# Fused attention and feed-forward block on Trainium2: three edits to which engine prepares the weights, the first softmax tiles and the first scale

## The chip, the cores and the metric

The kernel runs on one core of a Trainium2 chip. The core has a matrix engine (TensorE, PE in the profile, with its weight loads shown apart as PEld), three elementwise engines (VectorE or DVE, ScalarE or ACT, GpSimd or POOL) and a queue from which the DMAs are issued (SyncE or SP). Each engine runs its own instructions in the order in which they stand in its queue. The metric is the device time of one launch in microseconds; lower is better.

## What is computed

The reference, cut to what matters:

```python
scores = (1 / sqrt(64)) * q @ k.T            # q, k, v: 8 batches, 8 heads, 576 rows, 64 columns
thresh = max(scores, axis=-1) - tau
attn = exp(where(scores >= thresh, scores, -1e9) - max)
attn = attn / (sum(attn) + 1e-9)
x = (attn @ v), heads side by side           # 4608 rows of 512
h = x @ w_in                                 # 512 x 2048
out = (h * sigmoid(h)) @ w_out               # 2048 x 512
```

Everything is float32. The kernel gets the accuracy out of 16-bit products by carrying a number as a first part and a second part (the first rounded to float16, the second what the rounding left), and multiplying first by first, first by second and second by first. For that, weights, v and softmax weights are scaled by powers of two ahead of the split.

## The kernel before, in words

**Tiles.** The softmax works on tiles of 128 query rows by 576 keys. The program writes one loop over tile numbers t. In each step it writes the maximum of tile t (`soft1`, line 434, VectorE), the scores of tile t+1 (TensorE, line 412 or 424), the normalisation of tile t-1 (`soft2b`, line 466, ScalarE), the exponential of tile t (`soft1b`, line 444, ScalarE), what is done with the normalised tile t-1 (`soft3`), the tasks planned for step t, units of the feed-forward products, and the threshold, sum and reciprocal of tile t (`soft2`, lines 453, 457, 461, VectorE).

**Batch 0 in two halves.** Batch 0 is computed for the query rows 0 to 255 of each head first. These are 16 tiles, called direct tiles here (they are the visits of kind "low"): their scores, transposes (line 369) and products with v (`av_direct`, line 389) are done in float32 on TensorE. Then come twelve empty steps (`GAP`), then the other 20 tiles of batch 0 (kind "high"), then batches 1 to 7. All tiles but the direct ones are split into float16 parts: the first part by ScalarE up to step 36 (line 475) and by GpSimd after that (line 477), the second part by GpSimd (lines 480 and 483). A DMA then transposes both parts (line 493), and TensorE multiplies them with the split v (line 508).

**Weights.** There are 16 pieces of w_in and 16 of w_out, 128 rows by 512 columns each. They come as 64-bit words, are loaded into two staging buffers (w_in partly into eight other ones), and are decoded by ScalarE (line 191) and VectorE (lines 194 and 197). TensorE multiplies each decoded piece with itself (line 209); the largest entry of the sums bounds the square of the largest weight, and VectorE reads it (line 214). When all 16 pieces of a matrix have gone through this, `pow2_scales` turns the bound into a power of two (lines 111 to 149), and `split_weights` scales each piece (line 220, GpSimd), writes its first part (line 223, ScalarE) and its second (line 224, GpSimd). The parts of piece i lie where the raw piece i-2 lay, so that the split of piece i waits until that of piece i-2 is done.

**v.** v of a batch is loaded in four pieces (line 245). VectorE takes the largest absolute value of each (`vmax`, line 251), `pow2_scales` makes the scale (its square-root branch, lines 123 to 136, is for the weights alone), and `split_v` splits each piece (ScalarE line 288, VectorE line 289). From the scale of batch 0 also comes `xscale` (line 263), by which the direct products are scaled when they leave PSUM (lines 526 and 527).

**Feed-forward.** x is split and multiplied with w_in (`h_unit`, line 551); tanh, gate and split of the result run on ScalarE and VectorE (lines 559, 560, 566, 567); the product with w_out is `o_unit` (line 582), and the result leaves through ScalarE (line 592).

**What sets the order.** `at(step, task)` plans a task for a step. `W_PLAN` plans the weights: w_in is loaded and decoded in steps 0 to 10 and split in steps 10 to 12; w_out is decoded in steps 9 to 22 and split in steps 22 to 25, with a priority that puts its instructions ahead of 150 of the preceding ones. The framework then orders the instructions of each engine by priority and by the times of its own model of the chip; the order on the chip is fixed by that. So the position of an instruction in its engine's queue in the trace need not be that of its step. PSUM holds two score tiles, three banks for other products (two in rotation, one of which the weights' products and some scales use under the number 2), and one for the products with v.

Of the kernel before, what the change touches and what calls it, by code (L numbers as in the profile page):

```python
# [10 lines left out]
BF16 = mybir.dt.bfloat16  # L11
F32 = mybir.dt.float32
F32R = mybir.dt.float32r
I32 = mybir.dt.int32
AF = mybir.ActivationFunctionType
ALU = mybir.AluOpType
AX = mybir.AxisListType
PSUM = bass.MemoryType.PSUM

P = 128  # L20
# [3 lines left out]
NK = DM // P  # L24
# [28 lines left out]
def attention_moe(  # L53
# [10 lines left out]
    nc = tc.nc  # L64
    const = ctx.enter_context(tc.tile_pool(name="const", bufs=1))
# [12 lines left out]
    def bank(shape, name, own=None):  # L78
        if own is None:
            own = turn[0] = (turn[0] + 1) % turn[1]  # L80
        return ps_m.tile(shape, F32, tag=f"m{own}", name=name)
# [7 lines left out]
        out=gate, in0=tau_sb, scalar1=0.0, scalar2=0.125, op0=ALU.is_ge, op1=ALU.mult  # L89
# [3 lines left out]
        out=ntau, in0=tau_sb, scalar1=0.0, scalar2=-1.0, op0=ALU.max, op1=ALU.mult  # L93
# [6 lines left out]
    for i in range(2):  # L100
        t = const.tile([P, S + 64], F32R, name=f"qstack{i}")
# [4 lines left out]
    def pow2_scales(mx, name, own=None, squared=False):  # L106


        k = name[0]
        one = const.tile([P, 1], F32, name=f"{name}_one", tag=f"{k}_one")  # L110
        nc.vector.tensor_reduce(out=one, in_=mx, op=ALU.max, axis=AX.X)
        diag = const.tile([P, P], BF16, name=f"{name}_diag", tag="diag")
        nc.scalar.activation(diag, ident, AF.Copy, scale=one)
        allp = bank([P, P], f"{name}_ps", own)
        nc.tensor.matmul(allp, ones, diag, start=True, stop=True)
        one = const.tile([P, 1], F32, name=f"{name}_all", tag=f"{k}_all")
        nc.vector.tensor_reduce(out=one, in_=allp, op=ALU.max, axis=AX.X)
        cl = const.tile([P, 1], F32, name=f"{name}_cl", tag=f"{k}_cl")
        low, high = (2.0**-40, 2.0**94) if squared else (2.0**-20, 2.0**47)
        nc.vector.tensor_scalar(  # L120
            out=cl, in0=one, scalar1=low, scalar2=high, op0=ALU.max, op1=ALU.min
        )
        if squared:
            twice = const.tile([P, 1], F32, name=f"{name}_twice", tag=f"{k}_twice")
            nc.vector.tensor_scalar(
                out=twice, in0=cl, scalar1=2.0, scalar2=None, op0=ALU.mult
            )
            half = const.tile([P, 1], I32, name=f"{name}_half", tag=f"{k}_half")
            nc.vector.tensor_scalar(
                out=half, in0=twice.bitcast(I32), scalar1=1, scalar2=EXPMASK,  # L130
                op0=ALU.logical_shift_right, op1=ALU.bitwise_and,
            )
            cl = const.tile([P, 1], F32, name=f"{name}_root", tag=f"{k}_root")
            nc.vector.tensor_scalar(
                out=cl, in0=half.bitcast(F32), scalar1=2.0**64, scalar2=None, op0=ALU.mult
            )
        e2 = const.tile([P, 2], I32, name=f"{name}_e2", tag=f"{k}_e2")
        nc.vector.tensor_scalar(
            out=e2[:, 0:1], in0=cl.bitcast(I32), scalar1=EXPMASK, scalar2=None, op0=ALU.bitwise_and
        )  # L140
        nc.vector.tensor_scalar(
            out=e2[:, 1:2], in0=cl.bitcast(I32), scalar1=EXPMASK, scalar2=EXPMASK,
            op0=ALU.bitwise_and, op1=ALU.bitwise_xor,
        )
        sc = const.tile([P, 2], F32, name=f"{name}_sc", tag=f"{k}_sc", bufs=3)
        nc.vector.tensor_scalar(
            out=sc[:, 0:1], in0=e2[:, 1:2].bitcast(F32), scalar1=2.0**12, scalar2=None, op0=ALU.mult
        )
        nc.vector.tensor_scalar(
            out=sc[:, 1:2], in0=e2[:, 0:1].bitcast(F32), scalar1=2.0**-13, scalar2=None, op0=ALU.mult  # L150
        )
        return sc
# [4 lines left out]
    w16 = wst.bitcast(F16)  # L157
# [58 lines left out]
    def split_weights(i):  # L216
        w = wst[:, i + WSPARE, :]
        hi = w16[:, i, 0:512]
        sc = wsc["in" if i < 4 * NK else "out"][:, 0:1]
        nc.gpsimd.tensor_scalar(  # L220
            out=w, in0=w, scalar1=sc, scalar2=1.0, op0=ALU.mult, op1=ALU.mult
        )
        nc.scalar.activation(hi, w, AF.Copy)
        nc.gpsimd.tensor_tensor(
            out=w16[:, i, 512:1024], in0=w, in1=hi, op=ALU.subtract
        )
# [11 lines left out]
    vmx = {}  # L238
    vsc = {}
    v16 = {}  # L240
    vraw = {}

    def load_v(b, p):
        t = sb.tile([P, 2, 5, D], F32, tag="vraw", name=f"vraw_{b}_{p}", bufs=5)
        nc.sync.dma_start(out=t, in_=vL[b, :, 2 * p : 2 * p + 2])
        vraw[b, p] = t

    def vmax(b, p):
        if p == 0:
            vmx[b] = const.tile([P, NPAIR], F32, name=f"vmx_{b}", tag="vmx")  # L250
        nc.vector.tensor_reduce(
            out=vmx[b][:, p : p + 1], in_=vraw[b, p], op=ALU.max, axis=AX.XYZ,
            apply_absolute_value=True,
        )
# [3 lines left out]
    xscale = const.tile([P, 1], F32, name="xscale")  # L258

    def vscale(b):  # L260
        vsc[b] = pow2_scales(vmx[b], f"v{b}", (None, 2)[b] if b < 2 else 0)
        if b == 0:
            nc.vector.tensor_scalar(
                out=xscale, in0=vsc[0][:, 0:1], scalar1=2.0**-12, scalar2=None, op0=ALU.mult
            )
# [76 lines left out]
    direct = {}  # L342
    qzero = []
    for i in range(2):
        t = gbuf.bitcast(F32)[:, 4096 + 512 * i : 4608 + 512 * i]
# [55 lines left out]
    tiles = []  # L401
# [61 lines left out]
    def soft2b(t):  # L463
        w = wtile[t]
        r = small.pop(t)[:, 4:5]
        nc.scalar.activation(w, w, AF.Copy, scale=r)  # L466

    def soft3(t):
        if tiles[t][0] in direct:
# [162 lines left out]
    start = {}  # L632
# [38 lines left out]
    for b in range(B):  # L671
        u = start[b, 0]
        for p in range(NPAIR):
            if b == 0:
                at(-4, lambda p=p: load_v(0, p))
                at(0, lambda p=p: vmax(0, p))
                at(V_SLOT + p, lambda p=p: split_v(0, p))
            else:
                at(u + 9 * p - 40, lambda b=b, p=p: load_v(b, p))
                at(u + 9 * p - 34, lambda b=b, p=p: vmax(b, p))  # L680
                at(u + 9 * p + 4, lambda b=b, p=p: split_v(b, p))
        at(u - 2 if b else 1, lambda b=b: vscale(b))
# [16 lines left out]
    for first, t0, t1, t2, hp in W_PLAN:  # L699
        for i in range(16):  # L700
            ti = t0 + i * (t1 - t0) / 16
            at(math.floor(ti - 2), pri(hp, lambda i=i + first: load_weights(i)))
            at(math.floor(ti), pri(hp, lambda i=i + first: decode_weights(i)))
        at(t1, pri(hp, scale_out if first else scale_in))
        for i in range(16):
            at(t1 + i * (t2 - t1) // 16, pri(hp, lambda i=i + first: split_weights(i)))
# [26 lines left out]
    t = 0  # L733
    while t < NT + 8 or units or ready or held:
        while ready and ready[0][0] <= t:
            _, b, c0, n = ready.pop(0)
# [14 lines left out]
        if live(t - 1):  # L751
            soft2b(t - 1)
# [14 lines left out]
        for v, p, c0, n in avs.pop(t, []):  # L767
            b = visits[v][0]
# [5 lines left out]
            scale = xscale if v in direct else 2.0**-12  # L774
# [52 lines left out]
```

## Time and profile before

| | us |
|---|---|
| median of three runs | 1242.41 |
| lowest and highest | 1241.87, 1245.1 |
| the profiled execution, its own time | 1240.96 |
| span of the profile of that execution | 1238.8 |

The profile shows one execution. Its span runs from the first to the last instruction; 2.2 us of the execution's time lie outside. Engines are shown by their busy time; an instruction that waits for an input shows as idle time of its engine, and the trace names what released it. "x" is a count. PEclk is the granted clock of TensorE as a share of full speed. In a group of one source line, three numbers with slashes are the shortest, median and longest duration in ns.

The later stages look alike: from 250 us on TensorE is busy for more than 94% of each stretch, with softmax tiles of the batches 1 to 7 and feed-forward units side by side. The first 250 us hold everything that the change touches.

### The profile page before, as it was taken

The numbers are of one execution on the slowest core, as the hardware profiler recorded it, in microseconds if no ns is written. First come the engines' busy times: TensorE is split into PE (matmuls) and PEld (weight loads), VectorE is DVE, ScalarE is ACT, GpSimd is POOL, SyncE is SP. The second block draws the span as 40 slices with busy tenths as digits, with TensorE's granted clock in tenths as the row PEclk, the third lists the DMA queues.
The fourth block names the chain that finished last, engine by engine and source line by source line (L and its number), as shares of the span: only waits on it lengthen the run. The fifth ranks groups of instructions, "written<-read, shape, count | busy, mean of one in ns | idle before, by whom it ended". The sixth has DMA issues, their size and how long they took to land.

```text
span 1238.8 us, 26929 instructions
## 1 busy us (share of the span) xinstructions
PE 1142.8 (92%) x9402; PEld 896.8 (72%) x9402; DVE 931.1 (75%) x2603; ACT 814.8 (66%) x1507; POOL 748.6 (60%) x952
## 2 busy tenths in 40 slices
PE   5776766999899999999999999999999999999998
PEld 3544545777678778777777877787777877777777
DVE  7898866797989998989888859887689848333230
ACT  6888656687677867776777747776677847433331
POOL 1088999788678867886788618783688537200000
PEclk9997887999999999999999999999999999999999
DMA  9669556877878877788787648773688446200000
GB/s 303 183 208 207 129 98 131 158 135 151 163 129 151 160 150 146 154 144 162 141 153 148 123 99 146 157 148 88 118 162 154 83 79 112 52 15 15 14 12 24
DMA packets 363479, 158.15 MB, mean 128 GB/s; under 512 B 329552, under 2 KB 338256, under 8 KB 363344
## 3 DMA queue, kind: packets, MB, share of 16 engines
q1 hardware_dynamic: 363344, 156.43, 62.3%
q8 instruction: 74, 1.21, 0.4%
q14 instruction: 61, 0.50, 0.1%
HBM read 66.72 MB, written 9.44 MB: 61 GB/s over the span
## 4 chain that ended last, share of the span: by engine, by line
PE 64%; DVE 13%; DMA 8%; POOL 5%; ACT 5%; issue 3%; SPq 1%; POOLq 0%; ACTq 0%; DVEq 0%
PE h L551 23%; PE o L582 23%; PE s L424 10%; PE a L508 8%; DMA wT<-hl 3%; DVE w L453 3%; DVE sm L434 3%; DMA vraw<-in_vL 2%; DVE qstack L328 2%; POOL hl L480 2%; ACT w L444 2%; DVE v L289 1%; DMA wraw<-in_w_out 1%; POOL hl L477 1%; ACT w L466 1%
## 5 line engine op out<-in xcount | busy, mean ns | idle before, releaser
L551 PE MATMUL h<-x,wst 128*128 128x288 f16 (+2 forms) x3072 | 430.9, 289 | 14.0 <-DVE gbuf L567 12.0
L582 PE MATMUL o<-gbuf,wst 128*128 128x288 f16 (+2 forms) x3072 | 426.2, 288 | 4.9 <-ACT wst L592 2.5
L551 PEld LDWEIGHTS <-wst 128*128 128x128 f16 x3072 | 292.6, 99 | 102.8 <-issue 22.1
L582 PEld LDWEIGHTS <-wst 128*128 128x128 f16 x3072 | 294.5, 99 | 89.5 <-issue 9.1
L480 POOL TENSOR_TENSOR hl<-w,hl 128x512 f16<-128x512 f32 x272 | 325.3, 1196 | 15.7 <-DMA kraw<-in_kT 3.5
L477 POOL TENSOR_SCALAR hl<-w 128x576 f16<-128x576 f32 x264 | 178.8, 680 | 198.4 <-ACT w L466 128.3
L444 ACT ACTIVATE w<-s,sm 128x576 f32<-128x576 f32 x288 | 210.1, 737 | 81.4 <-DVE sm L434 33.8
L453 DVE SCALAR_TENSOR_TENSOR w<-s,sm,w 128x576 f32<-128x576 f32 x288 | 232.5, 812 | 41.4 <-ACT w L444 39.4
L466 ACT ACTIVATE w<-w,sm 128x576 f32<-128x576 f32 x288 | 218.4, 771 | 58.4 <-DVE sm L461 56.5
L434 DVE TENSOR_REDUCE sm<-s 128x1 f32<-128x576 f32 x288 | 215.0, 750 | 42.8 <-PE s L424 41.0
L560 DVE SCALAR_TENSOR_TENSOR h<-th,h 128x288 f32<-128x288 f32 (+2 forms) x256 | 116.5, 456 | 114.5 <-ACT th L559 112.0
L559 ACT ACTIVATE th<-h,msc 128x288 f32<-128x288 f32 (+2 forms) x256 | 126.9, 497 | 105.4 <-PE h L551 103.0
L424 PE MATMUL s<-khi,qstack 128*128 128x288 f32 x608 | 160.6, 346 | 31.3 <-DVE w L453 27.2
L566 ACT ACTIVATE gbuf<-h 128x288 f16<-128x288 f32 (+2 forms) x256 | 103.7, 407 | 81.6 <-DVE h L560 80.5
L567 DVE SCALAR_TENSOR_TENSOR gbuf<-h,gbuf 128x288 f16<-128x288 f32 (+2 forms) x256 | 114.9, 451 | 40.8 <-ACT gbuf L566 39.8
L508 PE MATMUL a<-wT,v 128*64 128x288 f16 (+1 forms) x1680 | 128.7, 295 | 10.2 <-DMA wT<-hl 10.2
L424 PEld LDWEIGHTS s<-khi,qstack 128*128 128x128 f32 x608 | 98.6, 197 | 53.8 <-issue 42.1
L338 POOL TENSOR_TENSOR klo<-kraw,khi 128x576 fp32r<-128x576 f32 x64 | 92.5, 1446 | 71.3 <-ACT khi L336 71.3
L424 PE MATMUL s<-klo,qstack 128*128 128x288 f32 x608 | 133.7, 302 | 0.0
L508 PEld LDWEIGHTS <-v 128*64 128x64 f16 x1680 | 91.3, 111 | 37.0 <-issue 25.0
L424 PEld LDWEIGHTS s<-klo,qstack 128*128 128x128 f32 x608 | 101.5, 196 | 0.5 <-issue 0.2
L483 POOL TENSOR_TENSOR hl<-w,hl 128x64 f16<-128x64 f32 x272 | 101.7, 374 | 0.0
(93 smaller groups left out, 830.6 us busy)
## 6 DMA issues: line engine op xcount, KB each, us to landing
qraw<-in_qT SPq DMA_DIRECT2D x128, 144.0 KB, 3.0
kraw<-in_kT SPq DMA_DIRECT2D x128, 144.0 KB, 3.1
vraw<-in_vL SPq DMA_DIRECT2D x32, 320.0 KB, 3.4
wraw<-in_w_out SPq DMA_DIRECT2D x16, 512.0 KB, 4.4
out_t<-wst SPq DMA_DIRECT2D x56, 144.0 KB, 2.2
wT<-hl SPq DMA_TRANSPOSE x304, 3.4
gbuf<-in_w_in SPq DMA_DIRECT2D x8, 512.0 KB, 7.5
wraw<-in_w_in SPq DMA_DIRECT2D x8, 512.0 KB, 6.0
```

The source lines that it names most:

```text
L424: nc.tensor.matmul(s_ps[:, j, :HALF], lhs, kk[:, j * HALF : (j + 1) * HALF], start=(n == 0), stop=(n == len(seq) - 1),)
L434: nc.vector.tensor_reduce(out=negm, in_=s_ps[:, :, :HALF], op=ALU.max, axis=AX.XY, negate=True)
L444: nc.scalar.activation(wtile[t].rearrange("p (j c) -> p j c", j=2), sps[t][:, :, :HALF], AF.Exp, bias=small[t][:, 0:1],)
L453: nc.vector.scalar_tensor_tensor(out=w3, in0=s_ps[:, :, :HALF], scalar=sm[:, 1:2], in1=w3, op0=ALU.is_ge, op1=ALU.mult, accum_out=sm[:, 2:3],)
L466: nc.scalar.activation(w, w, AF.Copy, scale=r)
L477: nc.gpsimd.tensor_scalar(out=fl[:, 0:S], in0=w, scalar1=1.0, scalar2=1.0, op0=ALU.mult, op1=ALU.mult)
L480: nc.gpsimd.tensor_tensor(out=fl[:, 640:1152], in0=w[:, 0:512], in1=fl[:, 0:512], op=ALU.subtract)
L508: nc.tensor.matmul(a_ps[odd * D : (odd + 1) * D, :n], vt[:, lo_v, odd, kv, :], wT[v, b * H + 2 * p + odd][:, kw, c0 - base : c0 - base + n ...
L551: nc.tensor.matmul(ph[:, :n], wi(c, f, lo_w), x16[b, lo_x][:, c, c0 : c0 + n], start=(k == 0), stop=(k == 11),)
L559: nc.scalar.activation(th[:, :n], ph[:, :n], AF.Tanh, scale=moe_sc[b][:, 0:1])
L560: nc.vector.scalar_tensor_tensor(out=ph[:, :n], in0=th[:, :n], scalar=1.0, in1=ph[:, :n], op0=ALU.add, op1=ALU.mult,)
L582: nc.tensor.matmul(ps[:, :n], wo(f, d, lo_w), g[:, lo_g, :n], start=(f == 0 and k == 0), stop=(f == NF - 1 and k == 2),)
```

## The change

It has three edits.

1. In `split_weights`, the pieces of w_out are no longer scaled by GpSimd. ScalarE writes the first part with the scale applied on the way, and VectorE writes the second part from the raw piece, the scale and the first part. The pieces of w_in keep the old three instructions.
2. In `soft2b`, the direct tiles (16 of batch 0) are normalised by GpSimd, in place, instead of ScalarE. All others stay.
3. In `vmax`, for batch 0, TensorE multiplies the upper halves of the words of v with themselves (20 products, into a PSUM bank under the number 2), and VectorE reduces the sum once; the four reductions over the pieces are gone. `vscale` for batch 0 takes the square-root branch of `pow2_scales`, three more small instructions. Batches 1 to 7 keep line 251.

No DMA is added, removed or planned for another step.

```diff
@@ split_weights
         sc = wsc["in" if i < 4 * NK else "out"][:, 0:1]
+        if i >= 4 * NK:
+            nc.scalar.activation(hi, w, AF.Copy, scale=sc)
+            nc.vector.scalar_tensor_tensor(
+                out=w16[:, i, 512:1024], in0=w, scalar=sc, in1=hi, op0=ALU.mult, op1=ALU.subtract
+            )
+            return
         nc.gpsimd.tensor_scalar(
             out=w, in0=w, scalar1=sc, scalar2=1.0, op0=ALU.mult, op1=ALU.mult
         )
@@ vmax
+    vps = []
+
     def vmax(b, p):
+        if b == 0:
+            if p == 0:
+                vps.append(bank([P, P], "vps_0", 2))
+            flat = vraw[b, p].rearrange("p o k d -> p (o k d)").bitcast(BF16)
+            upper = flat.rearrange("p (c t) -> p c t", t=2)[:, :, 1]
+            for j in range(5):
+                part = upper[:, j * P : (j + 1) * P]
+                nc.tensor.matmul(
+                    vps[0], part, part, start=(p == 0 and j == 0), stop=(p == 3 and j == 4)
+                )
+            if p == 3:
+                vmx[b] = const.tile([P, 1], F32, name="vmx_0", tag="vmx0")
+                nc.vector.tensor_reduce(out=vmx[b], in_=vps[0], op=ALU.max, axis=AX.X)
+            return
@@ vscale
-        vsc[b] = pow2_scales(vmx[b], f"v{b}", (None, 2)[b] if b < 2 else 0)
+        vsc[b] = pow2_scales(
+            vmx[b], f"v{b}", (None, 2)[b] if b < 2 else 0, squared=(b == 0)
+        )
@@ soft2b
-        nc.scalar.activation(w, w, AF.Copy, scale=r)
+        if tiles[t][0] in direct:
+            nc.gpsimd.tensor_scalar(
+                out=w, in0=w, scalar1=r, scalar2=1.0, op0=ALU.mult, op1=ALU.mult
+            )
+        else:
+            nc.scalar.activation(w, w, AF.Copy, scale=r)
```

## The prediction

> **What bounds the kernel now.** I read the page first, for the engines over the whole span and in 40 slices of 31 us.
>
> ```profile
> span 1238.8 us, 26929 instructions
> PE 1142.8 (92%) x9402; PEld 896.8 (72%) x9402; DVE 931.1 (75%) x2603; ACT 814.8 (66%) x1507; POOL 748.6 (60%) x952
> ...
> PE   5776766999899999999999999999999999999998
> ...
> DVE  7898866797989998989888859887689848333230
> ...
> POOL 1088999788678867886788618783688537200000
> PEclk9997887999999999999999999999999999999999
> ```
>
> TensorE is the bound as a whole, but not at the start: its first seven slices are below 8, its granted clock falls there too, and from the eighth slice on it is nearly full. The work of TensorE is the same before and after but for 20 small products. So what is saved in the first 250 us arrives at the end, because behind them TensorE has hardly a gap to lose it in. The windows of that start come next; the columns are the stretch, then busy time and count of PE, PEld, DVE, ACT and POOL, the clock, the DMA share and GB/s.
>
> ```profile
> 15.00:66.00 51.00, 40.35 (x237) 27.06 (x237) 47.45 (x138) 44.92 (x86) 3.42 (x3) 0.93 0.76 232
> 66.00:100.00 34.00, 22.23 (x141) 14.89 (x137) 30.82 (x77) 28.23 (x54) 32.71 (x35) 0.86 0.71 200
> 100.00:138.00 38.00, 28.96 (x208) 23.27 (x209) 31.37 (x91) 32.48 (x65) 34.39 (x35) 0.76 0.96 192
> 138.00:210.00 72.00, 45.88 (x315) 35.46 (x312) 48.91 (x129) 43.88 (x77) 68.45 (x82) 0.84 0.55 111
> 210.00:250.00 40.00, 34.74 (x290) 26.73 (x289) 31.32 (x87) 25.67 (x45) 31.11 (x42) 0.95 0.77 149
> 300.00:400.00 100.00, 94.26 (x779) 73.21 (x779) 90.10 (x258) 74.61 (x135) 75.86 (x99) 0.97 0.79 150
> ```
>
> There are two different stages. From 15 to 66 us, with the direct tiles, VectorE is busy 47.45 of 51 us (0.930), ScalarE 44.92, GpSimd almost not. From 138 to 210 us GpSimd is busy 68.45 of 72 us, and VectorE only 48.91. The chain of waits says the same of the second stage (start, us, what), with the timeline's row for the long run of GpSimd and the GpSimd time of lines 220 and 224 alone in that window:
>
> ```profile
> 137.13 0.93 POOL hl L480
> ...
> 142.02 7.97 POOL wst L220 x11
> ...
> 166.31 1.06 POOL hl L480
> 167.37 5.09 DMA wT<-hl
> ...
> 178.44 3.58 DVE v L289
> ...
> 217.63 4.98 DMA wT<-hl
> ```
>
> ```profile
> 142.00 11.79 POOL L220 TENSOR_SCALAR wst<-wst,o_w_sc 128x512 f32<-128x512 f32 x15
> ```
>
> ```profile
> 138.00:210.00 72.00, 12.48 (x16) 0.84 0.55 111
> ```
>
> ```profile
> 138.00:210.00 72.00, 18.29 (x16) 0.84 0.55 111
> ```
>
> From 137 to 167 us the chain hardly leaves GpSimd. In its middle stand 15 scalings of w_out in a row. They were released together by w_out's scale and went ahead of the float16 splits of the softmax tiles, for which the DMA transposes and then TensorE wait.
>
> **Edit 1, w_out.** It takes 12.48 + 18.29 = 30.77 us of GpSimd out of this stage, which leaves 68.45 - 30.77 = 37.68. ScalarE keeps its 16 first parts. VectorE gets 16 operations with two operands in SBUF. The trace has this form at line 197, of the same 512 elements, and at line 289 with 640. Line 194 has one operand. Each is shown here for the stretch in which GpSimd idles (0 to 66 us) and for a later one in which GpSimd is busy (66 to 138, for line 289 138 to 230); the three numbers are shortest, median and longest in ns:
>
> ```profile
> L194 DVE TENSOR_SCALAR wst<-wst x19: 405/416/428, 12.3 to 65.0; 128x512 int32<-128x512 int32 x19
> ```
>
> ```profile
> L194 DVE TENSOR_SCALAR wst<-wst x13: 404/753/1369, 68.5 to 125.2; 128x512 int32<-128x512 int32 x13
> ```
>
> ```profile
> L197 DVE SCALAR_TENSOR_TENSOR wst<-wraw,wst x11: 677/681/691, 21.5 to 65.5; 128x512 int32<-128x512 int32 x11
> ```
>
> ```profile
> L197 DVE SCALAR_TENSOR_TENSOR wst<-wraw,wst x14: 682/1089/1642, 65.5 to 125.7; 128x512 int32<-128x512 int32 x14
> ```
>
> ```profile
> L289 DVE SCALAR_TENSOR_TENSOR v<-vraw,v_sc,v x4: 869/870/874, 32.3 to 36.1; 128x640 f16<-128x640 f32 x4
> ```
>
> ```profile
> L289 DVE SCALAR_TENSOR_TENSOR v<-vraw,v_sc,v x4: 868/1272/3568, 143.3 to 199.3; 128x640 f16<-128x640 f32 x4
> ```
>
> So a second part costs VectorE between 0.681 and 1.089 us. GpSimd would be busy about 37.7 of some 65 us, 58%; 0.681 + 0.58 x 0.408 = 0.918, and 16 of them are 14.7 us (ends 10.9 and 17.4). Less GpSimd also gives something back: the four splits of v took 0.868 + 2 x 1.272 + 3.568 = 6.98 us, where undisturbed ones take 4 x 0.870 = 3.48, so 3.5 us go. VectorE then has 48.91 + 14.7 - 3.5 = 60.1 us of work and becomes the bound of the stage. How full can it be? Where it set the pace (15 to 66 us) it was 0.930 full: 60.1 / 0.930 = 64.6 us instead of 72, **7.4 us less**. The ends are 0.826 (31.37 of 38, from 100 to 138 us), which gives 72.8 and no gain, and 1, which gives 60.1 and 11.9 us. I take 0.930, because the stretch at 0.826 also had GpSimd 90% busy.
>
> The edit adds a wait: the ScalarE part of piece i waits for the VectorE part of piece i-2, and the VectorE part for the ScalarE part. Behind them in the two queues stand exponentials and tanh, and the maxima and gates; TensorE waits for these. The plan's priority puts all 16 early, so VectorE may run them as one block of some 15 us, as GpSimd does its 15 scalings now. In the sum that block is VectorE work like other work; its price beyond that is a rival below.
>
> From 210 to 250 us TensorE was 34.74 of 40 us busy, against 94.26 of 100 later. The chain still passes a DMA transpose at 217.63, late because the splits before it were late. At the later pace 34.74 would take 36.9: between 0 and 3.1 us, and I take **2.5 less**, as the cause goes away.
>
> **Edits 2 and 3, the direct tiles.** Their rows: the start of the timeline, and the groups of the operations concerned (busy us, mean ns of one).
>
> ```profile
> 6.22 2.45 DVE L251 TENSOR_REDUCE vmx<-vraw 128x1 f32<-128x640 f32 x3 [3.21 <-DMA vraw<-in_vL]
> ...
> 6.29 4.21 PE L412 MATMUL s<-kd,gbuf 128*128 128x288 f32 x8 [6.29 <-ACT gbuf L361]
> ...
> 10.78 1.41 DVE L434 TENSOR_REDUCE sm<-s 128x1 f32<-128x576 f32 x2
> ...
> 13.49 0.61 PE L209 MATMUL wps<-wst 128*128 128x128 bf16 x4 [2.99 <-DVE wst L197]
> ```
>
> ```profile
> 67.99 11.84 POOL L220 TENSOR_SCALAR wst<-wst,i_w_sc 128x512 f32<-128x512 f32 x15
> ```
>
> ```profile
> 78.39 0.76 ACT L466 ACTIVATE w<-w,sm 128x576 f32<-128x576 f32 x1
> ```
>
> ```profile
> L466 ACT ACTIVATE w<-w,sm 128x576 f32<-128x576 f32 x288 | 218.4, 771 | 58.4 <-DVE sm L461 56.5 <-DVE v_e L138 1.4
> ...
> L477 POOL TENSOR_SCALAR hl<-w 128x576 f16<-128x576 f32 x264 | 178.8, 680 | 198.4 <-ACT w L466 128.3 <-DMA wT<-hl 45.7 <-DVE h L560 17.8
> ...
> L214 DVE TENSOR_REDUCE wmx<-wps 128x1 f32<-128x128 f32 x8 | 2.2, 278 | 0.0
> ...
> L125 DVE TENSOR_SCALAR i_w_twice<-i_w_cl 128x1 f32<-128x1 f32 x1 | 0.1, 145 | 0.0
> ```
>
> *Scale of v.* The four reductions lie at 6.2 to 10.8 us, where VectorE otherwise waits for DMAs. Their going frees no saturated time, but the maxima of tiles 0 and 1 (1.41 us), queued behind them, can run while VectorE idles: between 0 and 1.4 less, I take **1.4**, since tile 0's scores are half of a TensorE run that starts at 6.29. Added on VectorE are one reduction of 0.278 and three small operations of 0.145: **0.7 more**. The 20 products take 5 x 0.61 = 3 us of TensorE at that early clock, with the next scores and the weights' products queued behind them and the same PSUM bank; before 13.5 us TensorE has nothing else due, so I cost them at nothing (3 us, if v lands later than that).
>
> *Normalisation.* ScalarE loses 16 x 0.771 = 12.3 us, GpSimd gets 16 of about 0.70 (line 477 takes 0.680 for as many elements). The tile's chain keeps its length. VectorE stays the pace of this stage, so ScalarE's relief can give no more than VectorE's idle time, 51 - 47.45 = 3.55 us. I take **2.3 less** (two thirds, ends 0 and 3.55). Against it stands what a busy GpSimd does to VectorE. By the medians above a decoded piece costs 0.337 + 0.408 = 0.745 us more, a split of v 0.402 more: 19 x 0.745 + 4 x 0.402 = 15.8 us if GpSimd were as full as from 66 to 138 us (67.1 of 72, 93%). About 15 normalisations in 51 us are 21%: 15.8 x 21 / 93 = **3.6 more** (ends 0 and 15.8).
>
> [...]
>
> *The last direct tiles.* In GpSimd's queue the normalisation stands with the splits of k and q of the next tiles and the 32 splits of w_in. Tile 15 is normalised at 78.39 now; GpSimd's run of 15 scalings ends at 79.83, and those are planned earlier. If tile 15 waits for it and then takes 0.7, it is done at 80.5 instead of 79.15: **1.4 more** (0 if it is queued ahead).
>
> No DMA changes its place. SyncE's queue only gains, its transposes waiting less for GpSimd.
>
> **Sum.** -7.4 - 2.5 - 1.4 + 0.7 - 2.3 + 3.6 + 1.4 = -7.9 us against the profiled execution, 1240.96 (span 1238.8): 1233.1. The median of the runs shown, 1242.41, lies 1.45 above it, so I forecast 1234.5 for the median.
>
> **Rivals.** *More is won (1224).* GpSimd's lag may be the cause of more than the busy sums tell: from 138 to 250 us TensorE is busy only 45.88 + 34.74 = 80.6 of 112. [...] For it speaks the unbroken GpSimd chain from 137 to 167; against it that beside a busy GpSimd VectorE stayed below 0.93 (30.82 of 34 and 31.37 of 38).
>
> *No change (1243).* VectorE takes GpSimd's place, runs w_out as one block, and the tiles are starved behind it: at 0.826 the stage takes 72.8, 0.8 more; with the other terms 0.3 more in all. For it speaks that the present block of 15 did just that to GpSimd; against it that VectorE has 23 us idle there.
>
> *Slower (1256).* GpSimd's normalisations stop VectorE where it is the bound. At the far end, 15.8 us in the direct stage, without ScalarE's relief, and second parts at 1.089 with the splits of v as slow as now: (48.91 + 17.4) / 0.930 = 71.3, only 0.7 less. In all -0.7 - 2.5 - 1.4 + 0.7 + 15.8 + 1.4 = 13.3 more. [...] Against it speaks that the threshold and sum (line 453), VectorE's longest softmax step, takes 807 ns in the direct stage and 812 over the whole span, so it does not mind GpSimd:
>
> ```profile
> L453 DVE SCALAR_TENSOR_TENSOR w<-s,sm,w x15: 793/807/818, 13.4 to 66.2; 128x576 f32<-128x576 f32 x15
> ```
>
> ```profile
> L453 DVE SCALAR_TENSOR_TENSOR w<-s,sm,w 128x576 f32<-128x576 f32 x288 | 232.5, 812 | 41.4 <-ACT w L444 39.4
> ```
>
> **How the numbers follow.** 0.3% of 1242.41 is 3.7 us, about what a measurement of this kernel tells from no change. Chances: forecast 0.44, more won 0.24, no change 0.18, slower 0.14. Faster takes the first but for a tail, and the second: 0.65; same 0.20; slower 0.15. The range reaches from past the second case, 1222, to 1247, where most of the slower case is left out. The forecast's own range is 1229 to 1241.
>
> **What would show it.** GpSimd without lines 220 and 224 at 138 to 200 us, at 55 to 65%; VectorE at 0.90 or more there with 16 operations near 0.92; TensorE's full stretch starting 6 to 12 us earlier. In the direct stage line 194 near 0.49 instead of 0.416 and the first maximum near 9 us. I am wrong if line 194 and 197 go to their later medians before 66 us, or if TensorE's idle time from 138 to 250 us does not shrink.

## The result and the profile after

| | before | after |
|---|---|---|
| median (us) | 1242.22 (4 runs, 1241.87 to 1245.1) | 1228.86 (4 runs, 1228.27 to 1229.98) |
| the profiled execution | 1240.96 | 1228.56 |
| its span | 1238.8 | 1226.8 |

The changed kernel takes 0.9888 of the time before, with a 95% interval of 0.9871 to 0.9906: 13.4 us less by the medians, 12.0 less by the spans. The forecast was 7.9 less, with 1229 to 1241 as its own range; the rival "more is won", at 1224 us, had 18 less. The measured time lies between the two: inside the prediction's whole range (1222 to 1247), and 0.1 us below the lower end of the forecast's own. In the runs further down, two single executions far above the rest (2916 us with edit 3 alone, 1921 us with edits 1 and 3) count in the medians but not in the ratios, which are estimated from the undisturbed ones and need not be the quotient of the two medians.

First the page of the changed kernel: the busy sums, and the slices of 31 us that changed most.

```profile
span 1226.8 us, 26991 instructions
...
PE   6867679999799999999999999999999999999998
...
DVE  6988998987888988988889958887789848332330
...
POOL 2289968786778778886888528872778447100000
PEclk9967889999999999999999999999999999999999
```

In the seventh slice (184 to 215 us) TensorE is at 9 where it was at 6, and from there on it is nearly full; the third and fifth are a tenth lower than before. The granted clock stands at 6 in the third slice, where it was 9, and at 9 in the seventh, where it was 7. The windows tell more (columns as before: stretch, then busy time and count of PE, PEld, DVE, ACT and POOL, then the clock, DMA share and GB/s).

```profile
15.00:66.00 51.00, 41.48 (x242) 26.85 (x242) 45.82 (x136) 36.75 (x71) 16.15 (x18) 0.90 0.77 230
66.00:100.00 34.00, 24.83 (x119) 16.22 (x117) 29.85 (x74) 24.32 (x45) 30.41 (x33) 0.60 0.68 198
100.00:138.00 38.00, 25.59 (x170) 20.38 (x169) 34.22 (x99) 33.94 (x67) 36.29 (x39) 0.78 0.80 190
138.00:210.00 72.00, 55.82 (x449) 44.62 (x448) 67.09 (x163) 52.67 (x91) 55.18 (x65) 0.88 0.68 143
210.00:250.00 40.00, 38.10 (x328) 29.22 (x323) 36.31 (x108) 31.30 (x57) 31.24 (x42) 1.00 0.73 148
```

From 138 to 210 us the roles have changed: VectorE is busy 67.09 of 72 us (0.932; the forecast said 0.930), GpSimd 55.18 instead of 68.45, and TensorE does 449 matmuls instead of 315. GpSimd is at 77% and not at the forecast's 55 to 65%, because more tiles pass through it: 20 of their long second parts (line 509) in this window, 14 before. In the stretch ahead of it TensorE does less: 119 + 170 = 289 matmuls from 66 to 138 us, where it did 141 + 208 = 349.

The chain of waits in that stage (start, us, what) had been GpSimd's. It is now VectorE's:

```profile
138.94 1.55 DVE v L313
...
140.56 2.27 DVE wst L222 x2
...
145.35 1.50 DVE wst L222
...
158.86 1.50 DVE wst L222
...
172.79 1.39 DVE wst L222 x2
...
```

Line 222 is the new second part of w_out. The rows also show that it stands singly or in pairs between softmax steps, and not as one block of 15.

The groups of one line (shortest, median and longest in ns, first and last start) answer to the prices in the prediction: the second parts, the normalisations on GpSimd, and two lines of the weights' decoding from 0 to 66 us.

```profile
L222 DVE SCALAR_TENSOR_TENSOR wst<-wst,o_w_sc x16: 736/782/1580, 140.5 to 173.4; 128x512 f16<-128x512 f32 x16
...
L491 POOL TENSOR_SCALAR w<-w,sm x16: 739/746/1502, 15.4 to 86.2; 128x576 f32<-128x576 f32 x16
...
L194 DVE TENSOR_SCALAR wst<-wst x18: 410/418/486, 13.5 to 63.2; 128x512 int32<-128x512 int32 x18
...
L197 DVE SCALAR_TENSOR_TENSOR wst<-wraw,wst x10: 673/682/691, 23.1 to 63.6; 128x512 int32<-128x512 int32 x10
```

The second parts took 15.13 us in all (the window's sum of that line), 0.946 each; the forecast had 0.918. Lines 194 and 197 did not move: medians 418 and 682 ns, 416 and 681 before. In the direct stage, these rows show nothing that VectorE paid for GpSimd's work.

The timeline (start, us, engine, line, what, count, and in brackets the idle time ahead and its releaser) shows what the change cost. First GpSimd at the end of the direct tiles, then the first product with w_in:

```profile
69.94 12.06 POOL L226 TENSOR_SCALAR wst<-wst,i_w_sc 128x512 f32<-128x512 f32 x15 [3.28 <-DVE i_w_sc L146]
81.98 2.71 POOL L230 TENSOR_TENSOR wst<-wst 128x512 f16<-128x512 f32 x2
84.68 0.68 POOL L226 TENSOR_SCALAR wst<-wst,i_w_sc 128x512 f32<-128x512 f32 x1
85.35 2.05 POOL L491 TENSOR_SCALAR w<-w,sm 128x576 f32<-128x576 f32 x2
...
97.17 0.72 PE L580 MATMUL h<-x,wst 128*128 128x256 f16 x5
```

The same first product before:

```profile
84.08 0.39 PE L551 MATMUL h<-x,wst 128*128 128x256 f16 x2
```

Two direct tiles, 14 and 15, stand behind w_in's 15 scalings and are normalised at 85.35 us, though their reciprocals (line 485) end at 73.41 and 74.91; ScalarE had done them at 68.38 and 78.39. Their products with v (line 413, from 92.64 to 97.24 in the chain of waits) come late, and so TensorE starts the feed-forward 13 us later. The forecast saw this wait, but only for tile 15 and at 1.4 us.

### The profile page after: what moved, and what is told of

It reads as the page before. It is cut to its first block, busy times and chain, and to the rows that moved or that the text cites. A ratio compares the mean times of both kernels' runs of the same rounds, so it can differ in the third digit from the quotient of the medians.

```text
span 1226.8 us, 26991 instructions
## 1 busy us (share of the span) xinstructions
PE 1145.4 (93%) x9422; PEld 898.1 (73%) x9422; DVE 934.2 (76%) x2619; ACT 808.6 (66%) x1491; POOL 739.4 (60%) x936
## 4 chain that ended last, share of the span: by engine, by line
PE 64%; DVE 16%; DMA 8%; ACT 5%; issue 3%; POOL 2%; SPq 1%; ACTq 0%; POOLq 0%; DVEq 0%
PE o L611 24%; PE h L580 22%; PE s L448 9%; PE a L537 7%; DVE w L477 4%; DVE sm L458 3%; DVE qstack L352 2%; DMA wT<-hl 2%; DMA vraw<-in_vL 2%; ACT w L468 2%; DMA wraw<-in_w_out 2%; ACT w L495 1%; DVE gbuf L596 1%; DMA kd<-in_kT 1%; DVE wst L222 1%
## 5 line engine op out<-in xcount | busy, mean ns | idle before, releaser
L611 PE MATMUL o<-gbuf,wst 128*128 128x288 f16 (+2 forms) x3072 | 420.0, 286 | 2.0 <-ACT wst L621 1.9
L495 ACT ACTIVATE w<-w,sm 128x576 f32<-128x576 f32 x272 | 205.7, 770 | 49.3 <-DVE sm L485 47.1
```

Of the source, the lines that this page charges most:

```text
L611: nc.tensor.matmul(ps[:, :n], wo(f, d, lo_w), g[:, lo_g, :n], start=(f == 0 and k == 0), stop=(f == NF - 1 and k == 2),)
```

## The experiments

The theory from the prediction is that GpSimd's work on w_out held the stage from 138 to 250 us, and that with this work gone VectorE sets the pace. The rivals are that GpSimd's load did not matter and the gain came from edits 2 or 3, and that what a busy GpSimd costs VectorE (line 194's median before: 753 ns beside a busy GpSimd, 416 beside an idle one) is as much as the relief brings. Ratios are to the kernel before, timed on the same chip, with 95% intervals; each group of four kernels shared one chip and one set of runs of the kernel before.

**Each edit by itself.** Edit 1 alone is the change to `split_weights` on the kernel before:

```diff
+        if i >= 4 * NK:
+            nc.scalar.activation(hi, w, AF.Copy, scale=sc)
+            nc.vector.scalar_tensor_tensor(
+                out=w16[:, i, 512:1024], in0=w, scalar=sc, in1=hi, op0=ALU.mult, op1=ALU.subtract
+            )
+            return
```

> Edit 1 alone on the kernel before. Theory G (the gain is GpSimd's relief from w_out between 138 and 210 us): 10 to 16 us less than before, about as much as all three edits (13.4 less). Rival S (the three edits each give a share, edits 2 and 3 some 4 to 6 us of it in the direct stage): 7 to 9 us less. Rival O (the gain is a luckier order of the queues, which any edit would shuffle): no relation, anywhere from 10 less to 5 more.

Measured: 1230.33 us against 1239.9, ratio 0.993 (0.9914 to 0.9946). That is 9.6 us less by the medians and 8.7 by the ratio, short of the 10 to 16 of the theory.

Edit 2 alone:

```diff
-        nc.scalar.activation(w, w, AF.Copy, scale=r)
+        if tiles[t][0] in direct:
+            nc.gpsimd.tensor_scalar(
+                out=w, in0=w, scalar1=r, scalar2=1.0, op0=ALU.mult, op1=ALU.mult
+            )
+        else:
+            nc.scalar.activation(w, w, AF.Copy, scale=r)
```

> Edit 2 alone (direct tiles normalised by GpSimd). Theory G: between no change and 5 us more, because the last two normalisations stand behind GpSimd's run of 15 scalings of w_in, as they do in the changed kernel (85.4 us instead of 78.4). Rival S: 2 to 4 us less, from ScalarE's relief. Rival O: anything.

Measured: 1245.12 us, ratio 1.0045 (1.0028 to 1.0063). Its window from 138 to 210 us is GpSimd's as before:

```profile
138.00:210.00 72.00, 49.24 (x359) 37.48 (x356) 49.79 (x132) 46.44 (x84) 68.88 (x82) 0.83 0.56 115
```

Edit 3 alone, the bound for v from TensorE:

```diff
     def vmax(b, p):
+        if b == 0:
...
+            for j in range(5):
...
+            return
...
-        vsc[b] = pow2_scales(vmx[b], f"v{b}", (None, 2)[b] if b < 2 else 0)
+        vsc[b] = pow2_scales(
+            vmx[b], f"v{b}", (None, 2)[b] if b < 2 else 0, squared=(b == 0)
+        )
```

> Edit 3 alone (v of batch 0 bounded by TensorE's products). Theory G: within 2 us of before; the first maximum moves from 10.78 us by a few tenths only, as it did in the changed kernel (10.56). Rival S: 1 to 3 us less. Rival O: anything.

Measured: 1239.44 us, ratio 1.0002 (0.9982 to 1.0021).

Edits 1 and 3, with the normalisation left on ScalarE:

```diff
-        if tiles[t][0] in direct:
-            nc.gpsimd.tensor_scalar(
-                out=w, in0=w, scalar1=r, scalar2=1.0, op0=ALU.mult, op1=ALU.mult
-            )
-        else:
-            nc.scalar.activation(w, w, AF.Copy, scale=r)
+        nc.scalar.activation(w, w, AF.Copy, scale=r)
```

> Edits 1 and 3 without edit 2. Theory G with the late normalisations as a cost: 13 to 18 us less than before, so equal to or up to 5 us better than the changed kernel. Rival S: 9 to 11 us less, so worse than the changed kernel by what edit 2 brought. Rival O: anything.

Measured: 1231.49 us, ratio 0.993 (0.9904 to 0.9955). That is 8.4 us less by the medians, below the range of the theory (13 to 18) and below that of rival S (9 to 11).

So only edit 1 pays by itself. Edit 2 alone costs 0.45%, edit 3 alone does nothing that can be measured. The three ratios add up to 0.23% less (-0.7 + 0.45 + 0.02), and yet the whole change gave 1.1% less. The next group times the whole change on the same chip as edits 1 and 2 together.

```diff
@@ split_weights
+            nc.scalar.activation(hi, w, AF.Copy, scale=sc)
+            nc.vector.scalar_tensor_tensor(
...
@@ soft2b
+        if tiles[t][0] in direct:
+            nc.gpsimd.tensor_scalar(
...
```

> Edits 1 and 2 without edit 3. Theory G (all of the gain is edit 1; 2 costs a little, 3 nothing): 0.993 to 0.998. Rival I (edit 2 costs alone, where GpSimd is the bound right after it, and gains once w_out has left GpSimd): 0.987 to 0.991, like all three.

Measured: 1237.54 us, ratio 0.997 (0.9954 to 0.9987). That is the sum of the two single edits (-0.7 + 0.45), near enough.

The changed kernel again, without an edit:

> The changed kernel once more, as the yardstick for the three others on the same chip. The first measurement gave 0.9888 of before. Edit 1 alone and edits 1 and 3 gave 0.993 on another chip, edit 2 alone 1.0045, so that the singles add up to 0.25% less and not 1.1%. If the edits really help each other, this run stays at 0.987 to 0.990; if the difference was one of chips and runs, it lies at 0.991 to 0.994.

Measured: 1231.05 us against 1240.83, ratio 0.9908 (0.9887 to 0.9929), between the two ranges expected. So edit 3, worth nothing alone, looks worth 0.6% on top of the other two. Where that lies is taken up below.

**GpSimd's load put back.** The changed kernel, with GpSimd made to do the two operations on 448 of the 512 columns of each piece of w_out again, into a tile that nothing reads:

```diff
+    spare = const.tile([P, 448], F32, name="spare")
...
             nc.vector.scalar_tensor_tensor(
                 out=w16[:, i, 512:1024], in0=w, scalar=sc, in1=hi, op0=ALU.mult, op1=ALU.subtract
             )
+            nc.gpsimd.tensor_scalar(
+                out=spare, in0=w[:, 0:448], scalar1=sc, scalar2=1.0, op0=ALU.mult, op1=ALU.mult
+            )
+            nc.gpsimd.tensor_tensor(
+                out=spare.bitcast(F16)[:, 0:448], in0=w[:, 0:448], in1=hi[:, 0:448], op=ALU.subtract
+            )
             return
```

> The changed kernel with GpSimd's two operations on each piece of w_out put back as useless work, on 448 of the 512 columns, into a spare tile; the outputs do not depend on it. VectorE and ScalarE do all that they do in the changed kernel. Theory G: GpSimd is the bound again from about 138 us, some 27 us of work in its queue: 9 to 16 us above the changed kernel, so at before's time or above it. Rival O (the gain is the order of the queues, not GpSimd's load): within 4 us of the changed kernel.

Measured: 1251.26 us, ratio 1.0069 (1.0045 to 1.0093), 20.2 us above the changed kernel on the same chip, more than the 9 to 16 expected. Its windows:

```profile
138.00:210.00 72.00, 51.38 (x356) 38.07 (x356) 66.30 (x153) 46.18 (x82) 67.33 (x77) 0.81 0.62 130
210.00:250.00 40.00, 28.46 (x173) 19.88 (x172) 32.27 (x82) 24.66 (x37) 40.00 (x51) 0.71 0.69 126
```

GpSimd is full again (40.00 of 40 us in the second row), and TensorE falls from 328 matmuls to 173 there. The added operations alternate between the two forms, so a block of 15 isn't needed for the loss. But this is more than a load. Nothing reads what GpSimd writes here, yet the added operations read the raw pieces, and the parts of a piece lie where an earlier raw piece lay. So each first part by ScalarE waits until GpSimd has read the piece two before: ScalarE's ninth begins at 188.47 us, GpSimd's seventh ends at 188.43. The second parts of w_out (now line 224) are drawn out to 248.5 us, where the changed kernel begins its last one at 173.4 and the kernel before at 208.7. Their group, and what TensorE waited for from 138 to 250 us (us in all, times, longest):

```profile
L224 DVE SCALAR_TENSOR_TENSOR wst<-wst,o_w_sc x16: 725/1241/1929, 142.0 to 248.5; 128x512 f16<-128x512 f32 x16
```

```profile
PE h L588 <- DVE gbuf L604: 9.9, 4, 3.5
PE s L456 <- DVE w L485: 9.4, 8, 2.3
PE o L619 <- ACT wst L223: 7.1, 5, 2.4
...
PE o L619 <- DVE wst L224: 1.4, 4, 0.4
```

For the late parts of w_out TensorE waited 7.1 + 1.4 = 8.5 us; in the kernel before it was 2.2 us, in the changed kernel none. VectorE is also as busy from 138 to 210 us as in the changed kernel (66.30 us), with fewer operations (153 for 163) and second parts of 1241 ns instead of 782. So the run shows that GpSimd's work on w_out costs much more than an order of the queues (some 5 us, below). It doesn't separate how: by the softmax splits queued behind it, by the late pieces of w_out, or by VectorE's slower operations.

Against the order as the cause speak also the counts of matmuls from 138 to 210 us in all profiled kernels. The five in which GpSimd works on w_out have 291 to 359 (before, edit 2, edit 3, this one, and the reordered kernel before, further down); the nine in which it doesn't have 405 to 456.

**The late tiles.** The changed kernel, with tiles 14 and 15 normalised by ScalarE as before:

```diff
-        if tiles[t][0] in direct:
+        if tiles[t][0] in direct and t < 14:
```

> The changed kernel, but tiles 14 and 15 are normalised by ScalarE as before; tiles 0 to 13 stay on GpSimd. In the changed kernel these two wait for GpSimd's run of 15 scalings of w_in until 85.4 us, instead of 68 and 78 us before. If that wait reaches the end: 2 to 6 us less than the changed kernel. If not (the time is made up where VectorE or the DMAs set the pace): within 2 us of it, with the first feed-forward products still some 6 us earlier.

Measured: 1225.23 us, ratio 0.9872 (0.9844 to 0.9899), 5.8 us below the changed kernel on the same chip. In its timeline the first product with w_in comes at 80.11 us:

```profile
67.29 11.93 POOL L226 TENSOR_SCALAR wst<-wst,i_w_sc 128x512 f32<-128x512 f32 x15 [3.02 <-DVE i_w_sc L146]
...
80.11 0.39 PE L580 MATMUL h<-x,wst 128*128 128x256 f16 x2
```

That is 17 us earlier than in the changed kernel (15 earlier than in its second profiled execution, which has 94.93), and 4 earlier than before. So the delay at the start of the feed-forward was not wholly hidden; about six of these us reached the end.

Another way to take w_in's scalings out of the tiles' way is to give them to VectorE:

```diff
         sc = wsc["in" if i < 4 * NK else "out"][:, 0:1]
...
-        nc.gpsimd.tensor_scalar(
+        nc.vector.tensor_scalar(
             out=w, in0=w, scalar1=sc, scalar2=1.0, op0=ALU.mult, op1=ALU.mult
         )
```

> The changed kernel with the scaling of w_in by VectorE in place of GpSimd, 16 operations of about 0.42 us (line 194's kind) instead of 16 of 0.8 us on GpSimd; the run of 15 scalings ahead of the high tiles is gone, though the second parts stay in GpSimd's queue there. If GpSimd is what holds the tiles at 66 to 138 us: 3 to 8 us less than the changed kernel. If VectorE holds them (busy 64 of 72 us there in the changed kernel): within 3 us of it or up to 4 us more.

Measured: 1229.3 us against 1240.01 (another chip), ratio 0.9921 (0.9903 to 0.9939): not told apart from the changed kernel. The tiles are late all the same, and now it is VectorE that holds them. Its scalings stand ahead of the sums and reciprocals of tiles 14 and 15, and the 16 take 13.95 us, 0.87 each where 0.42 was expected:

```profile
68.32 4.26 DVE L226 TENSOR_SCALAR wst<-wst,i_w_sc 128x512 f32<-128x512 f32 x6
...
72.83 5.65 DVE L226 TENSOR_SCALAR wst<-wst,i_w_sc 128x512 f32<-128x512 f32 x5
...
79.20 3.57 DVE L226 TENSOR_SCALAR wst<-wst,i_w_sc 128x512 f32<-128x512 f32 x4
...
85.87 0.15 DVE L485 RECIPROCAL sm<-sm 128x1 f32<-128x1 f32 x1
```

```profile
86.19 0.74 POOL L491 TENSOR_SCALAR w<-w,sm 128x576 f32<-128x576 f32 x1 [4.10 <-DVE sm L481]
```

GpSimd had nine second parts of w_in ahead of the two tiles, but was done with them and idle for 4.10 us before it could normalise tile 14.

**What an order is worth.** Every edit makes the framework order all queues anew. To see what that alone can do, two kernels change one priority number and nothing of the work. The kernel before:

```diff
-PRI_AV = 1500
+PRI_AV = 1510
```

> The kernel before with one priority of the plan moved from 1500 to 1510 (products with v), so that the order of the queues changes and no work does. It measures what an order alone is worth. If orders are worth little: within 0.2% of before. If the odd sums of the parts (0.993, 1.0045 and 1.0002 for one edit each, 0.989 to 0.991 for all three, 0.997 for edits 1 and 2) are orders: 0.3 to 0.6% either way.

Measured: 1241.38 us, ratio 1.001 (0.9992 to 1.0027). The changed kernel:

```diff
-PRI_S, PRI_SOFT1, PRI_SOFT2 = 1600, 50, 200
+PRI_S, PRI_SOFT1, PRI_SOFT2 = 1600, 55, 200
```

> The changed kernel with one priority moved from 50 to 55 (maximum and exponential); all work the same, nearly all queues in another order. Theory G, with orders worth little: 0.989 to 0.992 of before. If orders are worth 0.3 to 0.6%: outside of that, at 0.984 to 0.997, still below before.

Measured: 1232.84 us, ratio 0.9951 (0.9934 to 0.9969), where the changed kernel itself has 0.9908 (0.9887 to 0.9929). So another order moved the changed kernel by some 0.4%; its own two measurements, 0.9888 and 0.9908, differ by 0.2%. The same priority of 55 together with tiles 14 and 15 on ScalarE:

```diff
-PRI_S, PRI_SOFT1, PRI_SOFT2 = 1600, 50, 200
+PRI_S, PRI_SOFT1, PRI_SOFT2 = 1600, 55, 200
...
-        if tiles[t][0] in direct:
+        if tiles[t][0] in direct and t < 14:
```

> The variant with tiles 14 and 15 normalised by ScalarE (0.9872 of before), with the same shift of one priority from 50 to 55. If that variant's lead over the changed kernel comes from the two tiles no longer waiting: 0.985 to 0.989 again, and below the changed kernel in its other order. If it was an order: at 0.990 to 0.995.

Measured: 1223.28 us, ratio 0.9872 (0.9852 to 0.9892), the same as without the new number, and 9.6 us below the other kernel with this order. The gain of leaving tiles 14 and 15 on ScalarE shows in both orders (in the first the two intervals overlap a little, in this one they are apart), and this version has the lowest median of all kernels timed here.

**Where the gain is won and where it is lost.** The count of matmuls that TensorE has done by a given time shows how far one kernel is ahead of another. It is read from windows that start at 0. The kernel before:

```profile
0.00:138.00 138.00, 97.04 (x594) 68.65 (x595) 117.92 (x325) 111.58 (x212) 72.23 (x81) 0.88 0.81 218
0.00:250.00 250.00, 177.66 (x1194) 130.83 (x1195) 198.16 (x538) 181.13 (x332) 171.79 (x203) 0.88 0.73 176
0.00:600.00 600.00, 514.12 (x4042) 395.80 (x4043) 511.61 (x1434) 440.75 (x800) 439.35 (x545) 0.94 0.76 160
```

The changed kernel, whose counts hold the 20 new products of v:

```profile
0.00:138.00 138.00, 99.27 (x559) 68.89 (x560) 114.98 (x327) 100.44 (x190) 84.55 (x96) 0.80 0.76 216
0.00:250.00 250.00, 193.19 (x1328) 142.72 (x1329) 218.38 (x595) 184.40 (x337) 170.96 (x201) 0.86 0.73 184
0.00:600.00 600.00, 526.09 (x4148) 404.24 (x4149) 522.67 (x1470) 441.62 (x799) 440.10 (x543) 0.94 0.74 163
```

At 250 us the changed kernel is 1328 - 20 - 1194 = 114 matmuls ahead. The same subtraction for the profiled executions of the other kernels, at five times:

| matmuls ahead of before at | 138 us | 250 | 400 | 600 | 1150 | span against before (us) |
|---|---|---|---|---|---|---|
| edit 1 alone | -19 | 108 | 130 | 40 | 64 | -7.7 |
| edits 1 and 2 | -7 | 130 | 140 | 50 | 30 | -3.5 |
| edits 1 and 3 | -40 | 115 | 130 | 105 | 137 | -16.7 |
| the change | -55 | 114 | 113 | 86 | 99 | -12.0 |
| tiles 14 and 15 on ScalarE | 24 | 155 | 146 | 150 | 150 | -18.3 |
| the same, other order | 23 | 196 | 179 | 168 | 140 | -17.0 |
| GpSimd's load put back | -63 | -136 | -107 | -117 | -94 | 11.7 |

At 8.2 matmuls per us (99 ahead at 1150 us for 12.0 us at the end) the last two columns agree in every row, and I turn counts into us at that rate; the windows from 600 to 1150 us have 8.5 per us in both kernels. The counts treat all matmuls alike, and they differ between executions of one kernel: a second profiled execution of the changed kernel has 581 matmuls by 138 us, where this one has 559, and 2509 against 2494 by 400 us, so some 20 of them, 2.5 us, mean nothing.

Read so, all kernels of the table with edit 1 and without GpSimd's load are 108 to 196 matmuls ahead at 250 us, 13 to 24 us at 8.2 per us (the one with w_in scaled by VectorE, not in the table, is 97 ahead). They differ in what happens later. Edit 1 alone loses 90 of its 130 between 400 and 600 us, and edits 1 and 2 lose 90 of 140. In that stretch no edit has any instruction. Its windows, first of the kernel before, then of edit 1 alone:

```profile
400.00:500.00 100.00, 97.60 (x855) 77.99 (x855) 89.81 (x255) 73.87 (x136) 76.09 (x97) 1.00 0.78 149
500.00:600.00 100.00, 96.74 (x830) 77.12 (x829) 90.57 (x257) 73.06 (x133) 74.83 (x96) 1.00 0.77 146
```

```profile
400.00:500.00 100.00, 94.42 (x799) 74.68 (x797) 86.80 (x249) 71.67 (x131) 75.61 (x97) 0.98 0.79 148
500.00:600.00 100.00, 93.29 (x796) 75.11 (x795) 87.42 (x246) 70.27 (x128) 69.91 (x92) 0.98 0.73 142
```

TensorE idles 5.58 + 6.71 = 12.3 us there with edit 1 alone, 2.40 + 3.26 = 5.7 before. The waits of TensorE from 400 to 600 us (us in all, times, longest) say for what, with edit 1 alone and then in the changed kernel:

```profile
PE s L430 <- DVE w L459: 7.4, 5, 3.1
PE h L557 <- DVE gbuf L573: 2.8, 1, 2.8
PE o L588 <- ACT wst L598: 1.6, 1, 1.6
```

```profile
PE s L448 <- DVE w L477: 4.8, 4, 2.0
```

These are scores and feed-forward products that wait for steps of VectorE and ScalarE which no edit touches. Which of them come late may depend on where the softmax tiles and feed-forward units stand in the queues, but not on that alone: the second profiled execution of the changed kernel, in the same order, falls from 128 ahead at 400 us to 70 at 600. So the 0.6% between edits 1 and 2 and the whole change isn't shown to be edit 3's work: up to 400 us these two are 140 and 113 ahead, and the difference arises after that; it is no more than what an order or a single execution can be worth. That a queue's order is the cause of the stalls after 400 us was not tried by itself. The profiled execution of edits 1 and 3 was also the shortest of that kernel's (1223.87 us, against a median of 1231.49), so its row is at the good end; that of edit 1 alone was the longest (1232.88, against 1230.33).

## Why the prediction was right, point by point

**GpSimd's work on w_out holds the stage from 138 us: right.** Taking it away by itself gave 9.6 us, and putting it back cost 20.2. That it held the stage by the softmax splits alone, as the prediction's chain has it, isn't shown: in the 20.2 are also the late pieces of w_out (8.5 us of TensorE's waits) and perhaps VectorE's slower operations.

**Edit 1, -7.4 and -2.5: right in kind, too small.** VectorE became full at 0.932 where 0.930 was forecast. A second part took 0.946 us, forecast 0.918; the four splits of v took 862 + 2 x 1450 + 1662 ns = 5.4 us where 3.5 was forecast. By the counts edit 1 alone is 108 / 8.2 = 13.2 us ahead at 250 us, where the two terms had 9.9. The term that was too small can't be told from the counts. At 210 us edit 1 alone is already 97 ahead, but 92 of these are products with w_out, of which it has done 192 by 250 us, as many as the kernel before and the changed one. My reading is the cut at 210 us: I let VectorE set the pace up to there and took 210 to 250 by TensorE's pace, and in the trace VectorE is busy 67.09 + 36.31 = 103.4 of the 112 us from 138 to 250, 0.923. That is the picture of the rival "more is won": at 0.930 full, the forecast's 60.1 + 31.32 us of VectorE's work would take 98.3 of these 112 us, 13.7 less. The change does 114 + 55 = 169 matmuls more between 138 and 250 us, 21 us, of which 55 only make good what it lacked at 138. With tiles 14 and 15 on ScalarE nothing is lacking there, so most of the 55 is put down to them; but edits 1 and 3, which leave these tiles alone, are 40 behind there too.

**"What is saved in the first 250 us arrives at the end": right for the change, not in general.** Of 114 matmuls 99 arrive. With edit 1 alone it is 64 of 108: 13.2 us won by 250 us and (108 - 64) / 8.2 = 5.4 given back leave 7.8 in the profiled execution. That the medians give 9.6, so near the 9.9 forecast for it, is luck.

**What a busy GpSimd costs VectorE, +3.6 in the direct stage: wrong, it is near nothing.** The sign to look for was line 194 near 0.49 us; its median is 0.418 and its longest operation 0.486 (0.416 and 0.428 before). From 66 to 138 us, where GpSimd was busy 30.41 + 36.29 of 72 us, the same line has a median of 0.667. In the direct stage it was one of GpSimd's normalisations that took long, 1502 ns where their median is 746. I had scaled a price from stretches in which GpSimd was 93% busy to one in which it was 16.15 of 51 us busy, and the price did not scale so. Why so little of it came here was not tried.

**ScalarE's relief, -2.3: not seen at the end of the direct stage, and open after it.** ScalarE went from 44.92 to 36.75 us and VectorE from 47.45 to 45.82, but GpSimd's run of w_in's scalings, the end of that stage, began at 69.94 us instead of 67.99. In seven more profiles with the normalisation on GpSimd it began between 67.29 and 73.10, in five with all of it on ScalarE between 67.99 and 72.33. From 15 to 66 us the longest pieces of the changed kernel's chain are transfers:

```profile
15.46 8.82 DMA qraw<-in_qT
32.75 5.17 DMA kd<-in_kT
41.98 3.88 DMA wraw<-in_w_in
53.22 3.81 DMA kraw<-in_kT
61.66 4.38 DMA wraw<-in_w_out
```

VectorE at 0.93 was not the only limit of this stage; I read the fullest engine as the pace, and beside it stood loads, which take as long when ScalarE is relieved (median from issue to landing from 15 to 66 us: 8.3 us for q and 3.8 for k, 7.9 and 3.8 before). With tiles 14 and 15 on ScalarE, TensorE is 24 matmuls ahead at 138 us, 2.9 us, so some relief may arrive after this stage once the late tiles are gone. That kernel differs from edits 1 and 3 by the first 14 normalisations alone, and has 0.9872 (twice) against 0.993, some 7 us less. That is more than forecast, but hardly more than an order moved the time, so it isn't told apart from one.

**The first maxima, -1.4: wrong, 0.2.** They start at 10.56 us instead of 10.78. The queue was no longer in their way, but they waited for the scores:

```profile
10.56 1.42 DVE L458 TENSOR_REDUCE sm<-s 128x1 f32<-128x576 f32 x2 [7.54 <-PE s L436]
```

I had counted on tile 0's scores being half of a run that ends at 10.5; the trace releases the first maximum only when the run of both tiles has ended. The +0.7 for the added operations on VectorE and the products at no cost are not contradicted, but too small to be seen: edit 3 alone is within 0.2% of no change.

**Tiles 14 and 15, +1.4: right in kind, four to seven times too small.** Both tiles stood behind the run, not one, and behind two second parts more; the start of the feed-forward hung on them. Leaving them on ScalarE brought 5.8 and 9.6 us in two orders.

**The sum.** The errors went both ways. Edit 1 was worth 13.2 instead of 9.9 at 250 us, and GpSimd's work cost VectorE 3.6 less than forecast; against that, 1.2 + 2.3 us of small gains were not seen, and the late tiles cost 5.8 to 9.6 instead of 1.4. Put together as measured (the 0.7 as forecast), -13.2 - 0.2 + 0.7 + 5.8 is 6.9 us less, and 3.1 with 9.6. The change gave 13.4. So the terms taken one at a time don't add up to the whole; 6 to 10 us are left over, of which an order could explain some 5 (0.4%). The rest stays open. That the total came out within 6 us of the forecast is in part luck: errors of both signs offset each other. What is shown is where the main gain comes from (GpSimd's work on w_out), that the late tiles have a price, and that neither edit 2 nor edit 3 pays alone.

**The rivals.** "More is won" was nearer for the stage from 138 to 250 us (13.7, where edit 1 alone is 13.2 ahead by the counts); its 18 takes edits 2 and 3 at their good ends (-1.4 - 3.55 + 0.7, and nothing for a busy GpSimd), and these did not show. "No change" did not happen; the second parts went singly or in pairs between softmax steps, not as one block. "Slower" did not happen; its far end of 15.8 us met a cost near zero.

## What to carry to other kernels

When one engine's queue holds a stage, count what its work is worth over the whole stretch until the bound engine is full, not up to a cut inside it; putting a load back on the relieved engine is a cheap test of the cause, if the load neither reads nor writes a buffer that others wait for (here it did). Before a short step of a chain is moved to another engine, look at what its queue holds at the last of these steps: here 14 of 16 steps did no harm that was seen, and the last two stood behind 15 operations that nobody needed yet. Edits of half a per cent that reorder all queues can't be added up one by one; time the whole, and compare with a kernel in which only the order differs.

## What the runs showed of the hardware

From 15 to 66 us, fourteen GpSimd operations with float32 operands in SBUF left the medians of VectorE's lines 194 and 197 nearly as they were (418 and 682 ns, 416 and 681 before), and one of the fourteen took 1502 ns where their median is 746. From 138 to 210 us, with VectorE busy 67.09 and GpSimd 55.18 of 72 us, both had longer ones: a second part on VectorE had 736 ns at the shortest, 782 in the median and 1580 at the longest, and GpSimd's line 509 had a median of 1160 and a longest time of 1592. With GpSimd's load put back the median of the second part was 1241 ns.

The granted clock of TensorE in the stretch from 66 to 100 us was 0.60 in the changed kernel, 0.86 before. TensorE had 119 matmuls in it instead of 141. What made the clock fall was not tried.
